# Backward chain of a recurrent-memory attention block: token-major output gradient by PE transposes in place of a transposing DMA

## The chip, the cores and the metric

The kernel runs on one core of one Trainium2 chip. The time is device microseconds of that core, one execution at a time. One run of the kernel before, 4074.3 us, counted as slow and is left out of the ratios. The experiments ran on several chips (11, 12 and 14 are on record); each ratio is to executions of the kernel before on the same chip in the same rounds. Readings by segment come from one profiled execution of each kernel.

The profile's names: PE is TensorE, which does the matmuls, PEld its weight loads, DVE is VectorE, ACT ScalarE, POOL GpSimd, and SP SyncE, which here only issues DMA. SBUF and PSUM are the core's memories; matmuls leave their results in PSUM, and an *evacuation* is the copy from there to SBUF. A `q` after an engine's name (SPq) is what its sequencer issues. The *span* is the time from the first to the last instruction.

## The reference

The reference computes one transformer block and all its gradients. The part that matters is the attention, which runs over 64 segments of 32 tokens, each with 8 memory rows that come from the segment before (cut to what matters):

```python
for s in range(n_seg):                                   # 64 segments, L = 8 + 32 = 40 rows
    h = jnp.concatenate([mem, xs], axis=1)
    q, k, v = (jnp.einsum('btd,dhe->bhte', h, W) for W in (Wq, Wk, Wv))   # 16 heads of 256
    p = _softmax(jnp.where(mask, (q @ k^T) * scale, -1e9))
    o = jnp.einsum('bhte,hed->btd', p @ v, Wo)
    mem = o[:, :M, :].copy()                             # goes to the next segment
```

So the backward pass is a chain as well: the gradient of segment s needs the memory gradient that segment s+1 leaves. Outputs are the block's result and nine gradients, within a tolerance on bf16 data.

## The kernel before

The kernel has four stages: forward chain (0 to about 1370 us), feed-forward (to about 1760), backward chain (to about 3200) and a tail that forms the weight gradients. One segment of the backward chain, in the order of the source (cuts marked with `...`; numbers are the lines that the profile shows):

```python
# 732: output gradient, head-major, 128 matmuls in 4 PSUM tiles
nc.tensor.matmul(pss[b][:, jj*L:(jj+1)*L], lhsT=WoT_sb[...], rhs=do_roll[:, kc, sl, :], ...)
for b in range(4):                                       # 75 on DVE, 77 on ACT
    k.evac(doT[:, 8*b:8*b+8, 0:L], ..., "vsvs"[b])
# 737: dO_sb, the token-major copy (transpose) of doT, two halves, by DMA on SP's queue
for hf in range(2):
    nc.sync.dma_start_transpose(out=dO_sb[:, 8*hf:8*hf+8, :],
                                in_=doT[:, 16*hf:16*hf+16, :].rearrange("p c n -> p (c n)"))
# 744: dP = dO V^T;  748 to 753: softmax gradient dS on DVE
# 711: three passes of 16 matmuls: "v" (needs dO_sb), "k" (needs dS, Q_sb), "q" (needs dS^T, K_sb)
# 761: 16 small transposes dS -> dS^T, before the "k" pass
# 775: 32 matmuls after each pass that add to the memory gradient
# 778 to 793: the memory gradient goes to do_roll for the next segment
...
if r == 0:       # r = s % 4; s falls, so this is the last of a tile of four segments
    for nm in "kqv":
        nc.gpsimd.dma_start(out=dr["X_" + nm][t], in_=blk[nm]...)   # 1 MB each
        nc.gpsimd.dma_start(out=dr["M_" + nm][t], in_=lo[nm]...)    # 0.25 MB each
    # 806 (96 matmuls), 811 and 817 (fp32, 4 each): DXN of the tile, off the chain
```

Every segment also loads V, Q and K of the next one with transposing DMAs (lines 683 to 685) on the same SP queue, each into a single buffer. The instructions of an engine are ordered by a scheduler when the kernel is built, so the order on PE is not simply that of the source. Below, "remainder r" means segments with s % 4 = r. The tile's stores are issued at remainder 0 and are on their way during the following segment, remainder 3.

## Time and profile before

| | before |
|---|---|
| median time | 4040.6 us (3 runs, 4034.8 to 4063.8) |
| backward chain, mean segment | 22.1 us |
| its granted PE clock, 1800 to 3180 us | 0.83 |
| PE idle in front of L711 for the transposing DMA | 176 us of 1380 |

The last row is the longest of PE's waits in that stretch (who waited for whom: us in total, times, longest):

```profile
PE psf L711 <- DMA arA<-arA: 176.0, 82, 17.5
```

From the page of the kernel before: busy time, the granted clock in 40 slices (tenths), the chain that ended last (by engine, then by line), and the group of the value pass (busy and mean; after the last bar, idle time before it and what ended it).

```profile
PE 3250.6 (81%) x54460; PEld 2063.5 (51%) x54526; DVE 1366.3 (34%) x2969; ACT 840.1 (21%) x2053; POOL 524.2 (13%) x1129
...
PEclk9999999998998699968888878788888888899999
...
PE 63%; DMA 19%; DVE 5%; issue 5%; SPq 4%; ACT 3%; POOL 1%; ACTq 0%; DVEq 0%; POOLq 0%
PE psf L382 11%; DMA arA<-arA 10%; PE po L775 10%; PE psf L899 7%; PE psf L732 4%; PE po L466 4%; PE psf L711 3%; PE fx L806 2%; PE psf L423 2%; ACT arA L77 2%; PE psf L569 2%; PE fx L495 2%; PE psf L782 2%; PE fx L904 2%; PE fx L363 2%
...
L711 PE MATMUL psf<-arB,arA 128*128 128x80 bf16 x1024 | 79.5, 243 | 194.6 <-DMA arA<-arA 194.3
```

`DMA arA<-arA` is the transpose from one SBUF place to another: doT to dO_sb. It holds 10% of the whole span, and practically all the idle time in front of the value pass is put down to it.

The busy times by stretch of the kernel before, for the body of the backward chain (columns: stretch, length, busy PE, PEld, DVE, ACT, POOL, then granted clock, DMA share, GB/s):

```profile
1800.00:3180.00 1380.00, 1107.20 (x22150) 718.88 (x22150) 465.96 (x1119) 293.38 (x916) 175.35 (x416) 0.83 0.75 148
```

The timeline of one segment of the kernel before (remainder 1; start, length, engine, line, then in brackets the idle time before it):

```profile
2443.25 4.21 PE L732 MATMUL psf<-arA,arW 128*128 128x40 bf16 x128 [0.28 <-DVE arA L786]
...
2445.87 3.36 SPq L737 DMA_TRANSPOSE arA<-arA  x2
...
2447.39 0.94 PE L744 MATMUL psf<-arA 128*64 128x40 bf16 x32
...
2448.95 0.46 PE L711 MATMUL psf<-arB,arA 128*128 128x80 bf16 x8 [0.62 <-DMA arA<-arA]
...
2449.99 0.74 PE L775 MATMUL po<-arW,arA 128*32 128x448 bf16 x9 [0.58 <-DVE arA L75]
...
2451.97 0.72 PE L711 MATMUL psf<-arB,arA 128*128 128x80 bf16 x8 [1.23 <-DMA arA<-arA]
```

PE ends the score-gradient matmuls at 2448.3 us, and the second half of the value pass starts at 2452.0. In between it has 17 matmuls to do.

The queue of SP in the kernel before, where a tile's stores are on their way (remainder 3 starts at 2484.7 us):

```profile
2481.61 7.90 SPq L685 DMA_TRANSPOSE arW<-KT  x1
2489.62 1.86 SPq L737 DMA_TRANSPOSE arA<-arA  x1
...
2492.90 1.46 SPq L737 DMA_TRANSPOSE arA<-arA  x1
```

The K load takes 7.9 us to be issued once, and the output gradient stands behind it.

Two measures recur below. Both are worked out from the instructions in the trace: the *period* of a segment, from the start of its first L732 matmul to that of the next segment's, and the *key start*, from the end of the last L732 matmul to the start of the first L711 matmul of the key pass. They are means over the segments that start after 1800 us.

### The profile page before, as it was taken

The numbers are of one execution on the slowest core, as the hardware profiler recorded it, in microseconds if no ns is written. First come the engines' busy times: TensorE is split into PE (matmuls) and PEld (weight loads), VectorE is DVE, ScalarE is ACT, GpSimd is POOL, SyncE is SP. The second block draws the span as 40 slices with busy tenths as digits, with TensorE's granted clock in tenths as the row PEclk, the third lists the DMA queues.
The fourth block names the chain that finished last, engine by engine and source line by source line (L and its number), as shares of the span: only waits on it lengthen the run. The fifth ranks groups of instructions, "written<-read, shape, count | busy, mean of one in ns | idle before, by whom it ended". The sixth has DMA issues, their size and how long they took to land.

```text
span 4023.1 us, 120689 instructions
## 1 busy us (share of the span) xinstructions
PE 3250.6 (81%) x54460; PEld 2063.5 (51%) x54526; DVE 1366.3 (34%) x2969; ACT 840.1 (21%) x2053; POOL 524.2 (13%) x1129
## 2 busy tenths in 40 slices
PE   4888988898888488838888788778887857899899
PEld 2666666666665365625555555445555523333444
DVE  3433443443343266713333333233333223110101
ACT  2222222222222132302222222122221100111100
POOL 3111111111111111111111111111111111000000
PEclk9999999998998699968888878788888888899999
DMA  7445444544543877897778776777787789867742
GB/s 258 154 147 170 155 147 157 162 150 145 175 142 125 198 181 177 203 228 141 151 148 160 166 142 149 131 140 149 153 156 167 203 270 184 178 137 155 182 167 83
DMA packets 1156999, 662.58 MB, mean 165 GB/s; under 512 B 1045316, under 2 KB 1075828, under 8 KB 1148740
## 3 DMA queue, kind: packets, MB, share of 16 engines
q1 hardware_dynamic: 1070148, 392.73, 47.7%
q0 software_dynamic: 58976, 238.56, 16.9%
q10 hardware_dynamic: 27360, 23.58, 2.0%
q8 instruction: 427, 7.00, 0.7%
q14 instruction: 88, 0.72, 0.1%
HBM read 124.49 MB, written 270.64 MB: 98 GB/s over the span
## 4 chain that ended last, share of the span: by engine, by line
PE 63%; DMA 19%; DVE 5%; issue 5%; SPq 4%; ACT 3%; POOL 1%; ACTq 0%; DVEq 0%; POOLq 0%
PE psf L382 11%; DMA arA<-arA 10%; PE po L775 10%; PE psf L899 7%; PE psf L732 4%; PE po L466 4%; PE psf L711 3%; PE fx L806 2%; PE psf L423 2%; ACT arA L77 2%; PE psf L569 2%; PE fx L495 2%; PE psf L782 2%; PE fx L904 2%; PE fx L363 2%
## 5 line engine op out<-in xcount | busy, mean ns | idle before, releaser
L75 DVE CAST arA<-psf 128x320 bf16<-128x320 f32 (+6 forms) x1093 | 498.5, 481 | 1246.7 <-PE psf L711 346.9
L77 ACT CAST arA<-psf 128x480 bf16<-128x480 f32 (+6 forms) x1139 | 442.8, 407 | 1883.8 <-PE psf L711 383.5
L775 PE MATMUL po<-arW,arA 128*32 128x448 bf16 x6144 | 442.6, 410 | 44.8 <-DVE arA L75 34.9
L382 PEld LDWEIGHTS <-arW 128*128 128x128 bf16 x16384 | 438.3, 98 | 30.8 <-issue 18.6
L382 PE MATMUL psf<-arA,arW 128*128 128x40 bf16 x16384 | 440.3, 182 | 16.2 <-issue 9.9
L732 PE MATMUL psf<-arA,arW 128*128 128x40 bf16 x8192 | 227.3, 183 | 62.2 <-POOL arA L680 37.8
L775 PEld LDWEIGHTS <-arA 128*32 128x32 bf16 x6144 | 163.0, 105 | 202.0 <-DVE arA L75 64.2
L732 PEld LDWEIGHTS <-arW 128*128 128x128 bf16 x8192 | 225.8, 98 | 77.4 <-issue 72.5
L899 PE MATMUL psf<-arW,arA 128*128 128x512 bf16 x990 | 258.5, 391 | 7.9 <-ACT arA L77 7.9
L899 PEld LDWEIGHTS <-arA 128*128 128x128 bf16 x1440 | 138.5, 100 | 206.8 <-issue 66.3
L711 PE MATMUL psf<-arB,arA 128*128 128x80 bf16 x1024 | 79.5, 243 | 194.6 <-DMA arA<-arA 194.3
L569 PE MATMUL psf<-arA,arW 128*128 128x256 bf16 x1344 | 167.4, 287 | 75.3 <-DMA arA<-arA 40.5
L75 DVE CAST arB<-psf 40x320 bf16<-40x320 f32 (+2 forms) x256 | 92.4, 361 | 310.5 <-PE psf L457 145.9
L569 PEld LDWEIGHTS <-arW 128*128 128x128 bf16 x1344 | 138.3, 103 | 106.4 <-issue 80.6
L711 PEld LDWEIGHTS <-arA 128*128 128x128 bf16 x1024 | 58.5, 123 | 254.6 <-DMA arA<-arA 232.1
L363 PE MATMUL fx<-arW,arA 128*128 128x512 bf16 x456 | 121.6, 388 | 58.0 <-DMA arW<-in_A_Wv_dram 39.0
L920 PE MATMUL psf<-arW 128*128 128x448 bf16 x450 | 103.0, 382 | 64.0 <-DVE arA L75 53.8
L466 PE MATMUL po<-arW,arB 128*8 128x448 bf16 x2048 | 149.0, 448 | 2.8 <-DVE arB L75 0.3
L423 PE MATMUL psf<-arW,arB 128*32 128x512 bf16 x2048 | 148.7, 381 | 1.2 <-issue 1.2
L806 PE MATMUL fx<-arW,arA 128*32 128x448 bf16 x1536 | 142.2, 396 | 0.0
L920 PEld LDWEIGHTS <-arW 128*128 128x128 bf16 x606 | 61.8, 103 | 129.8 <-issue 70.9
L457 PE MATMUL psf<-arB,arA 128*128 128x80 bf16 x1024 | 56.1, 217 | 89.3 <-DMA arA<-arA 73.8
(355 smaller groups left out, 3846.8 us busy)
## 6 DMA issues: line engine op xcount, KB each, us to landing
QT<-arA POOLq DMA_DIRECT2D x64, 512.0 KB, 3.8
KT<-arA SPq DMA_DIRECT2D x64, 512.0 KB
VG<-arA SPq DMA_DIRECT2D x64, 512.0 KB
X_o<-arA POOLq DMA_DIRECT2D x40, 512.0 KB, 4.8
Vx<-arA POOLq DMA_DIRECT2D x32, 512.0 KB, 3.2
arA<-Vx SPq DMA_DIRECT2D x128, 128.0 KB
X_v<-arA POOLq DMA_DIRECT2D x16, 1024.0 KB, 5.9
X_k<-arA POOLq DMA_DIRECT2D x16, 1024.0 KB, 8.0
```

What stands on the lines that cost most here:

```text
L75: nc.vector.tensor_copy(out=out, in_=in_)
L77: nc.scalar.copy(out=out, in_=in_)
L363: nc.tensor.matmul(pv[:, 0:512], lhsT=hx_b[t % 2][:, kc, :], rhs=Wv_sb[:, kc, n * 512:(n + 1) * 512], start=(kc == 0), stop=(kc == KC - 1))
L382: nc.tensor.matmul(pss[b][:, jj * L:(jj + 1) * L], lhsT=W_sb[:, kc, c * P:(c + 1) * P], rhs=hT_roll[:, kc, sl, :], start=(kc == 0), stop=( ...
L423: nc.tensor.matmul(pV[b][32 * j:32 * j + 32, 0:512], lhsT=memT_pad[:, kc, :], rhs=Wv_sb[:, kc, n * 512:(n + 1) * 512], start=(kc == 0), st ...
L466: nc.tensor.matmul(pO[32 * (j % 4):32 * (j % 4) + M, 0:D], lhsT=o8[:, j, :], rhs=Wo_sb[:, cj(j), :], start=(j < 4), stop=(j >= MC - 4), sk ...
L569: nc.tensor.matmul(ps[:, f2 * 256:(f2 + 1) * 256], lhsT=Wt[:, kc, c * P:(c + 1) * P], rhs=xT[:, kc, :], start=(kc == 0), stop=(kc == KC - 1))
L711: nc.tensor.matmul(ps[b][:, i * 2 * L:(i + 1) * 2 * L], lhsT=lhs[:, cl, :], rhs=rhs_bd[:, cl // 2, :, :].rearrange("p g n -> p (g n)"), st ...
L732: nc.tensor.matmul(pss[b][:, jj * L:(jj + 1) * L], lhsT=WoT_sb[:, kc, c * P:(c + 1) * P], rhs=do_roll[:, kc, sl, :], start=(kc == 0), stop ...
L775: nc.tensor.matmul(pH[32 * (j % 4):32 * (j % 4) + 32, 0:D], lhsT=blk[nm][:, j, r * SEG:(r + 1) * SEG], rhs=WT[:, cj(j), :], start=(wi == 0 ...
L806: nc.tensor.matmul(px[32 * (j % 4):32 * (j % 4) + 32, 0:D], lhsT=lo[nm][:, j, :], rhs=WT[:, cj(j), :], start=(wi == 0 and j < 4), stop=(wi ...
L899: nc.tensor.matmul(pa[2 * kc + g][:, 0:w], lhsT=lhs_of(b)[:, kc * P:(kc + 1) * P], rhs=rhs_of(b, g), start=(b == 0), stop=(b == nblk - 1), ...
```

## The change

The intent is to take the DMA out of the segment's chain: PE transposes doT itself, 8 blocks of 128x128 a half, into a PSUM tile of bf16, and ACT copies the tile to dO_sb. The consumers do not change.

```diff
-            for hf in range(2):
-                nc.sync.dma_start_transpose(out=dO_sb[:, 8 * hf:8 * hf + 8, :],
-                                            in_=doT[:, 16 * hf:16 * hf + 16, :].rearrange("p c n -> p (c n)"))
+
+            def token_major(hf):
+                ph = k.ps1()[:].bitcast(BF16)
+                for i in range(8):
+                    c0 = 2 * (8 * hf + i)
+                    nc.tensor.transpose(ph[:, i * P:(i + 1) * P], doT[:, c0:c0 + 2, :].rearrange("p c n -> p (c n)"), ident[:, :])
+                nc.scalar.copy(out=dO_sb[:, 8 * hf:8 * hf + 8, :], in_=ph.rearrange("p (c n) -> p c n", n=P))
+            token_major(0)
             pD = k.ps1()
             ...                       # 744 before, 749 after: the score-gradient matmuls
+            token_major(1)
```

Lines after the change move by 4 to 6: L744 becomes L749, L761 L767, L775 L781; the transposes are L741, their copies L742. L711 and L732 stay.

## The prediction

> **What bounds the kernel now.** 4040.6 us. The backward chain runs from about 1760 to 3200 us: 64 dependent segments, averaging 22.1 us. From 1800 to 3200 us the busy times by stretch show PE busy 1124 of 1400 us, a granted clock of 0.76 to 0.87 and a DMA share of 0.74 to 0.78. The chain of waits puts "DMA arA<-arA" at 10% of the span, and the groups show PE idle 194 us before L711 for that DMA. It is the transpose of the output gradient: its two halves are issued at L737 after the evacuations of L732, and the value pass (L711) needs them. From the timeline, the key pass starts 14.4, 10.7, 8.2, 8.3 us (means) after a segment's last L732 matmul, for segment number mod 4 of 3, 2, 1, 0. Remainder 3 is worst: the transposes queue behind the K load (7.9 us to issue once) while 3 MB of X_k, X_q and X_v are stored.
>
> **Removed.** Two DMA transposes a segment, 128 in all: about 2048 of some 8470 small packets a segment (an estimate: 3.2 us of the 16 engines). Their waits before L711 go.
>
> **Added.** 16 PE transposes a segment, like those of L883 in the tail (33.0 us for 384, so 86 ns each): 1.4 us of PE. Two ACT copies of 128x1024 bf16 from PSUM, 1.01 us each at L77 in the tail: 2.0 us of ACT, which is 21% busy. The shared PSUM tag gets two more users; I expect no stall there.
>
> **The new path**, after the last L732 matmul: 0.7 us transposes, 0.95 score-gradient matmuls, 0.7 transposes; the second copy ends near 3.4 us; the value pass ends near 4.0. The changed instruction order then has all 32 L775 matmuls (1.7 us) and the 16 dS transposes (0.6), so the key pass starts near 6.3 us. DVE has dS ready by about 5.2, before PE wants it. The rest of a segment (2.8 + 5.0 + 3.4 us) stays: 17 to 18 us for a plain one. Saved: about 2.2 us at remainders 0 and 1, 2.7 at remainder 2 (the DXN matmuls move later), 6.5 at remainder 3, keeping some stall for the K load. Mean 3.4 us over 63 segments: 215 us.
>
> **Clock.** The Trainium skill, "TensorE: Matmul & The Clock Gate", Part 1, has PE fall to half rate after idle windows of about 3.4 us; this trace agrees: its clock records are only 1.0 or 0.5, in multiples of 3.4 us, and segments at 0.91 lasted 18.2 to 20.3 us against 19.0 to 20.4 near 0.75. I expect 0.88 to 0.92 here; Part 4 says transposes do not count as busy, which could hold that back.
>
> **Predicted time:** 3822 us, 8 in 10 between 3760 and 3895. Faster by over 2%: 0.94; within 2%: 0.04; slower: 0.02.
>
> **What would show it.** The DMA entry leaves the top of the chain of waits; the key pass starts 6 to 6.6 us after L732 in plain segments; segments average 18.3 to 19 us; transposes take 60 to 90 ns, copies 1.0 us; q1 moves a quarter less in this stage; the backward granted clock rises; other phases stay within 10 us.
>
> **What would make it wrong.** The store burst at remainder 3 may delay the K, V or next-tile loads, returning part of the 6.5 us as another DMA wait; two ACT copies in a row may delay later evacuations; the clock may stay near 0.82; or less DMA traffic and a clock near 1 save more.

## The result

The changed kernel takes 3815.3 us (4 runs, 3808.7 to 3829.7), against 4037.7 for the kernel before on the same chip. The ratio is 0.9448, 95% interval 0.9391 to 0.9506: 5.5% faster. (A ratio is the mean time of one kernel's fast runs over that of the other's of the same rounds, so it is not quite the ratio of the medians quoted.)

From the page of the changed kernel, the same parts, and the group of the new copies:

```profile
PE 3141.8 (83%) x55484; PEld 2052.6 (54%) x55550; DVE 1350.1 (35%) x2969; ACT 960.6 (25%) x2181; POOL 522.8 (14%) x1129
...
PEclk9999999999998869996999989999999789999999
...
PE psf L382 11%; PE po L781 8%; PE psf L905 8%; PE psf L732 5%; PE po L466 4%; DMA arA<-arA 3%; PE psf L711 3%; PE psf L569 2%; PE fx L812 2%; PE psf L423 2%; PE fx L495 2%; PE fx L910 2%; PE fx L363 2%; PE psf L741 2%; PE psf L788 2%
...
L742 ACT COPY arA<-psf 128x1024 bf16<-128x1024 bf16 x128 | 129.5, 1012 | 55.6 <-PE psf L741 54.0
```

The DMA fell from 10% to 3% of the chain; what is left of that name belongs to other SBUF-to-SBUF transposes. PE has a thousand matmuls more and yet is busy 109 us less: the same matmuls take longer when the clock is lower. The 128 of L732 take 4.21 us in the segment shown of before, where the granted clock was half for 3.4 us, and 3.35 us in the one below, at full clock. The busy times by stretch, body of the backward chain, changed kernel:

```profile
1800.00:2954.00 1154.00, 996.15 (x23052) 707.24 (x23052) 450.20 (x1118) 409.86 (x1038) 174.61 (x415) 0.94 0.79 150
```

The clock rose from 0.83 to 0.94. The body is 226 us shorter (1380 to 1154): by these two lines PE is idle 115 us less and busy 111 us less. So about half of the gain came as shorter waits and half as less busy time, of which the higher clock is at least a part. No run here takes the waits away and keeps the clock low, so the two are not separated by experiment. The timeline of a plain segment of the changed kernel (remainder 1 again):

```profile
2359.90 3.35 PE L732 MATMUL psf<-arA,arW 128*128 128x40 bf16 x128
...
2363.10 0.61 PE L741 MATMUL psf<-ident,arA 128*128 128x128 bf16 x8
...
2363.63 0.69 PE L749 MATMUL psf<-arA 128*64 128x40 bf16 x32
2363.80 1.01 ACT L742 COPY arA<-psf 128x1024 bf16<-128x1024 bf16 x1
...
2364.26 0.62 PE L741 MATMUL psf<-ident,arA 128*128 128x128 bf16 x8
...
2364.86 0.46 PE L711 MATMUL psf<-arB,arA 128*128 128x80 bf16 x8
...
2364.97 1.01 ACT L742 COPY arA<-psf 128x1024 bf16<-128x1024 bf16 x1 [0.16 <-PE psf L741]
...
2366.03 0.46 PE L711 MATMUL psf<-arB,arA 128*128 128x80 bf16 x8 [0.71 <-ACT arA L742]
...
2366.43 1.70 PE L781 MATMUL po<-arW,arA 128*32 128x448 bf16 x32
```

The second half of the value pass starts 2.8 us after L732; in the segment shown of before it was 4.5. The only wait left in this piece is 0.7 us for the second ACT copy.

Where the time went, by remainder (mean periods in us):

| remainder | before | after | saved | saving predicted |
|---|---|---|---|---|
| 3 (the tile's stores on their way) | 26.4 | 24.3 | 2.1 | 6.5 |
| 2 | 22.4 | 16.7 | 5.7 | 2.7 |
| 1 | 19.7 | 16.2 | 3.5 | 2.2 |
| 0 | 19.9 | 16.7 | 3.2 | 2.2 |
| all | 22.1 | 18.4 | 3.7 | 3.4 |

From the first segment's start to the last one's, the chain took 1416.9 us before (1760.2 to 3177.2) and 1188.2 us after (1765.8 to 2954.0), 228.7 us less. The profiled spans differ by 216.5 us, since the chain begins 5.6 us later and what follows takes 6.7 us more.

The remainder-3 segments are the surprise: they kept nearly all their length. PE's waits in the body of the chain, changed kernel (who waited for whom: us in total, times, longest):

```profile
PE psf L732 <- issue: 39.2, 8, 12.7
PE psf L749 <- issue: 25.8, 3, 11.6
PE psf L711 <- ACT arA L742: 23.4, 34, 1.0
...
PE psf L741 <- issue: 8.8, 3, 4.6
PE psf L711 <- DMA arW<-QT: 5.7, 2, 4.1
...
PE psf L711 <- DMA arW<-KT: 3.9, 2, 3.1
```

The old wait of 176 us for the transposing DMA is gone. In its place, and at remainder 3 alone, stand stalls marked "issue": PE waits for nothing that the profile shows. One of them in the timeline of the changed kernel, at remainder 3, with SP's queue beside it:

```profile
2239.14 18.80 SPq L685 DMA_TRANSPOSE arW<-KT  x1
...
2244.92 0.94 PE L749 MATMUL psf<-arA 128*64 128x40 bf16 x27
...
2257.37 0.35 PE L749 MATMUL psf<-arA 128*64 128x40 bf16 x5 [11.52 <-issue]
...
2258.04 5.16 SPq L683 DMA_TRANSPOSE arA<-VG  x1
```

PE stops between two like matmuls of one group, after 27 of 32. The matmuls just before the stop already read the last quarter of doT, and V comes in one load, so an operand is hardly what it waits for there. Three facts of the trace point to the fetch of PE's own instructions. First, counting PE's instructions (weight loads too, and of a matmul and its load the one that starts first) from the start of the trace, 18 of the 23 PE gaps over 0.9 us in this stage end at a position that leaves the same remainder, 137, when divided by 256; the other five stand at a named operand. Second, each of the 18 ends 1.2 to 1.6 us after a 16 KB packet of the instruction queue landed, but for one, which ends 3.8 us after. Third, in front of the gap shown no packet of that queue starts between 2236.2 and 2254.8 us, where the 180 of this stage come 6.4 us apart on average; 180 times 256 is 46,080, and PE with its weight loads has 46,104 instructions there, so this queue carries PE's. The 18 add up to 82 us. The Trainium skill, "Runtime: NRT & Kernel Launch", section "Instruction fetch mechanics", says that instructions are refilled in 16 KiB blocks of 256 by a DMA queue of the sequencer's own, and that crossing a block is "mostly hidden". The block size agrees with this trace; "mostly hidden" does not hold while the stores are on their way. In the kernel before, such gaps add up to 21 us in 6 places: PE stood still at remainder 3 for the output gradient anyway (93 us of the 176).

### The profile page after: what moved, and what is told of

Its sections match the earlier page's. It is cut to its first block, busy times and chain, and to the rows that moved or that the text cites. A ratio compares the mean times of both kernels' runs of the same rounds, so it can differ in the third digit from the quotient of the medians.

```text
span 3806.6 us, 122548 instructions
## 1 busy us (share of the span) xinstructions
PE 3141.8 (83%) x55484; PEld 2052.6 (54%) x55550; DVE 1350.1 (35%) x2969; ACT 960.6 (25%) x2181; POOL 522.8 (14%) x1129
## 3 DMA queue, kind: packets, MB, share of 16 engines
q0 software_dynamic: 58976, 238.56, 18.4%
## 4 chain that ended last, share of the span: by engine, by line
PE 65%; DMA 14%; issue 7%; DVE 5%; SPq 4%; ACT 4%; POOL 1%; ACTq 0%; DVEq 0%; POOLq 0%
PE psf L382 11%; PE po L781 8%; PE psf L905 8%; PE psf L732 5%; PE po L466 4%; DMA arA<-arA 3%; PE psf L711 3%; PE psf L569 2%; PE fx L812 2%; PE psf L423 2%; PE fx L495 2%; PE fx L910 2%; PE fx L363 2%; PE psf L741 2%; PE psf L788 2%
## 5 line engine op out<-in xcount | busy, mean ns | idle before, releaser
L781 PE MATMUL po<-arW,arA 128*32 128x448 bf16 x6144 | 334.2, 360 | 42.5 <-DMA arW<-in_A_Wv_dram 21.2
L732 PE MATMUL psf<-arA,arW 128*128 128x40 bf16 x8192 | 225.7, 182 | 90.2 <-POOL arA L680 39.3
L732 PEld LDWEIGHTS <-arW 128*128 128x128 bf16 x8192 | 223.2, 98 | 107.1 <-issue 102.2
L905 PE MATMUL psf<-arW,arA 128*128 128x512 bf16 x990 | 260.8, 393 | 12.7 <-ACT arA L77 12.7
L905 PEld LDWEIGHTS <-arA 128*128 128x128 bf16 x1440 | 138.7, 100 | 213.6 <-issue 73.4
L781 PEld LDWEIGHTS <-arA 128*32 128x32 bf16 x6144 | 149.2, 97 | 176.4 <-DVE arA L75 44.1
L742 ACT COPY arA<-psf 128x1024 bf16<-128x1024 bf16 x128 | 129.5, 1012 | 55.6 <-PE psf L741 54.0
L457 PE MATMUL psf<-arB,arA 128*128 128x80 bf16 x1024 | 57.9, 221 | 97.3 <-DMA arA<-arA 77.5
L812 PE MATMUL fx<-arW,arA 128*32 128x448 bf16 x1536 | 121.8, 368 | 1.5 <-issue 1.5
L495 PE MATMUL fx<-arW,arA 128*128 128x448 bf16 x512 | 120.7, 362 | 0.0
```

What stands on the lines that cost most here:

```text
L495: nc.tensor.matmul(px[:, 0:D], lhsT=xblk[:, j, :], rhs=Wo_sb[:, cj(j), :], start=(j == 0), stop=(j == MC - 1))
L732: nc.tensor.matmul(pss[b][:, jj * L:(jj + 1) * L], lhsT=WoT_sb[:, kc, c * P:(c + 1) * P], rhs=do_roll[:, kc, sl, :], start=(kc == 0), stop ...
L781: nc.tensor.matmul(pH[32 * (j % 4):32 * (j % 4) + 32, 0:D], lhsT=blk[nm][:, j, r * SEG:(r + 1) * SEG], rhs=WT[:, cj(j), :], start=(wi == 0 ...
L812: nc.tensor.matmul(px[32 * (j % 4):32 * (j % 4) + 32, 0:D], lhsT=lo[nm][:, j, :], rhs=WT[:, cj(j), :], start=(wi == 0 and j < 4), stop=(wi ...
L905: nc.tensor.matmul(pa[2 * kc + g][:, 0:w], lhsT=lhs_of(b)[:, kc * P:(kc + 1) * P], rhs=rhs_of(b, g), start=(b == 0), stop=(b == nblk - 1), ...
```

## The experiments

Two questions: what of the change made the gain, and what holds remainder 3. For the first, the theory is latency: the DMA's way from doT to dO_sb was on the chain. Its rivals are the DMA traffic that the change takes away, the clock that busier PE keeps up, and the new instruction order that the scheduler makes.

### Dead DMA: the old traffic kept, without its latency

Edit on the changed kernel; nothing reads `spare`, which is free memory:

```diff
+            for hf in range(2):
+                nc.sync.dma_start_transpose(out=spare[:, 8 * hf:8 * hf + 8, :],
+                                            in_=doT[:, 16 * hf:16 * hf + 16, :].rearrange("p c n -> p (c n)"))
             def token_major(hf):
```

> The changed kernel, plus the two old DMA transposes of each segment into spare memory that nothing reads. Theory (the latency of the transposing DMA sat on the critical path): the time stays near the changed kernel's 3815 us, 3810 to 3880, plain segments (number mod 4 of 0 to 2) stay at 16.0 to 16.9 us; any loss falls in the remainder-3 segments. Rival (the gain came from less DMA traffic and a shorter SP queue): most of the 222 us is lost, 3960 to 4040 us, and plain segments go back to 18 us or more.

Measured: 3815.7 us (4 runs), ratio 0.9448 (0.9384 to 0.9511), the same as the changed kernel. Plain segments take 16.1 to 16.8 us, remainder 3 25.3. The stretch shows that the traffic was there, with a DMA share of 0.99 in place of 0.79:

```profile
1800.00:2960.00 1160.00, 988.35 (x22656) 696.00 (x22655) 442.54 (x1097) 401.60 (x1016) 173.07 (x411) 0.93 0.99 177
```

So taking some 3.2 us of DMA work (the prediction's estimate) out of each segment was worth nothing by itself, within the 0.6% that the interval leaves. The traffic rival falls.

### Dead PE work: the change's cost without its use

The mirror image, on the kernel before: the two DMA transposes stay and are waited for, and `token_major` writes `spare`.

```diff
+            # as in the change, but:
+                nc.scalar.copy(out=spare[:, 8 * hf:8 * hf + 8, :], in_=ph.rearrange("p (c n) -> p c n", n=P))
```

> The kernel before, plus the change's 16 PE transposes and two ACT copies a segment into spare memory that nothing reads; the value pass still waits for the DMA. PE's instruction order is then nearly that of the changed kernel. Theory (latency): no gain, 4010 to 4090 us, PE still idles over 150 us in front of L711 for the DMA. Rival (the added PE work keeps the clock up, or the new instruction order is what helps): 3820 to 3950 us and a backward clock of 0.9 or more.

Measured: 3976.4 us, ratio 0.9854 (0.9807 to 0.9900). This is a miss: 1.5% faster, where I expected nothing; the rival's 3820 to 3950 us did not come either. The wait for the DMA is all there, as PE's waits show for this run (stretch 1800 to 3100 us):

```profile
PE psf L712 <- DMA arA<-arA: 176.5, 95, 13.9
```

The granted clock rose to 0.89 in this stretch, from 0.83, with the wait still there. So busier PE and a higher clock, without an end of the wait, brought no more than these 1.5% here.

By remainder the gain is 3.3 us at 2 (22.4 to 19.1), 0.5 and 0.9 at 1 and 0, and none at 3. So about 60 of the 222 us do not come from the latency. Two causes of these 60 us remained: PE work or clock, or instruction order.

### One, two, three dead transposes: when the order changes

The same edit with N transposes and N*128 columns copied a half, in place of 8. With N=1 the order is nearly that of the kernel before. With N=2 the four fp32 transposes of DXN (L817 of before), which stand between the key pass and its rows in all 15 tiles, move behind the query pass, and one of the four DXN sums (L811) moves behind the dS transposes; four more of the L806 matmuls stand at remainder 2, in front of the second half of the value pass (15 in place of 11). From N=3 on the dS transposes follow all the value-pass rows, as in the changed kernel.

> The kernel before, plus 1 unused PE transpose and a 128-column ACT copy a half. The run with 2 gained 1.5%, nearly all at remainder 2 (22.4 to 19.9 us), where its instruction order has the four L817 transposes of DXN split and moved towards the next segment; with 1 transpose these stand in all 15 tiles where the kernel before has them, in front of the key pass's rows. If the place of the DXN work is the cause: no gain, 4015 to 4045 us, remainder 2 at 21.8 us or more. If any unused PE work does it (or the two more users of the PSUM tag): 3960 to 3995 us, remainder 2 near 20.

> The kernel before, plus 2 unused PE transposes (not 8) and a 256-column ACT copy for each half. With this little work the scheduler keeps the old instruction order (value-pass rows split around the dS transposes). If the 60 us that the run with all the unused work gained came from the new instruction order: no gain here, 4020 to 4060 us. If it came from the PE and ACT work as such (a busier PE, a higher clock): a part of it, 4005 to 4025 us.

> The same with 3 unused transposes a half: 6 of 16, but the scheduler now joins the dS transposes behind all the value-pass rows, as in the changed kernel. If instruction order is the cause: 3980 to 4005 us, and the step from 2 to 3 transposes is 20 to 50 us. If the PE work is the cause: within 12 us of the run with 2.

| N | ratio to before | 95% interval | remainder 2 |
|---|---|---|---|
| 1 | 0.9977 | 0.9938 to 1.0016 | 21.7 us |
| 2 | 0.9853 | 0.9817 to 0.9888 | 19.9 us |
| 3 | 0.9889 | 0.9857 to 0.9921 | 20.0 us |
| 8 | 0.9854 | 0.9807 to 0.9900 | 19.1 us |

(Medians 4022.2, 3968.4, 3985.5 and 3976.4 us.) The run with 2 went against what was written for it: I held it to be the old order, having looked only at the value-pass rows. Then I found that DXN had moved, and wrote the expectation of the run with 1 on that: it held for the time, and remainder 2 came out at 21.7 us, just under the 21.8 written. The run with 3 fell in its range, but the step of 20 to 50 us between 2 and 3 did not come (17 us the other way).

The step lies between 1 and 2, where PE's work hardly changes and the place of DXN does; more dead work adds nothing, and neither does joining the dS transposes. The order in which PE takes off-chain work is therefore the likely cause of the 60 us, mostly in the remainder-2 segment, where the end of DXN stands. The last column is from single executions, for N=2 the slowest of its six (4010.7 us) and for N=1 the fastest (3997.4), so the ratios weigh more.

How the order acts is not fully taken apart. In the traces PE idles 0.7 us less in a remainder-2 segment with N=2: L811's wait of 0.6 us for ACT is gone, and the wait for the DMA is no shorter (1.6 us before, 1.7 with N=2). The rest of the 2.4 us is less busy time: the clock rose there from 0.82 to 0.94.

### One half by DMA, the other by PE

```diff
 # e5: first half as in the change; in place of token_major(1), right after token_major(0):
+            nc.sync.dma_start_transpose(out=dO_sb[:, 8:16, :], in_=doT[:, 16:32, :].rearrange("p c n -> p (c n)"))
 # e6: second half as in the change; in place of token_major(0):
+            nc.sync.dma_start_transpose(out=dO_sb[:, 0:8, :], in_=doT[:, 0:16, :].rearrange("p c n -> p (c n)"))
```

> The changed kernel with the second half of the gradient (head chunks 8 to 15) made by the DMA transpose again, the first half by PE. Same DMA traffic as the next run. Theory (what counts is when each half arrives): this half is issued last, right after the last evacuation, so PE waits for it in every segment: plain segments 17 to 18.5 us in place of 16.0 to 16.9, remainder 3 back towards 25 to 27 us, total 3880 to 3965 us. Rival (cost in proportion to the DMA work): half of the gain lost, about 3925 us, in both half runs alike.

> The mirror image: first half by DMA, second half by PE. Theory: the first half is issued some 1.4 us before PE ends L732 and its latency hides behind the score-gradient matmuls and the remaining transposes; plain segments within 0.5 us of the changed kernel's 16.0 to 16.9; at remainder 3 the DMA still queues behind the K load, which adds some us there; total 3820 to 3895 us, clearly below the other half run. Rival: the same time as the other half run.

| | changed | second half DMA | first half DMA |
|---|---|---|---|
| median us | 3815.3 | 3911.6 | 3940.2 |
| ratio to before | 0.9448 | 0.9715 | 0.9756 |
| remainder 3 | 24.3 | 24.5 | 29.0 |
| remainder 2, 1, 0 | 16.7, 16.2, 16.7 | 18.6, 18.7, 18.4 | 17.5, 17.0, 17.5 |

The totals are alike, as the traffic rival had it, but the segments are not. With the second half by DMA every plain segment is about 2 us longer and remainder 3 no worse (I had written 25 to 27 us for it). There PE waits 60 us for the DMA, but its stalls marked "issue" fall from 85 to 25 us: one wait covers the other, as in the kernel before. With the first half by DMA the plain segments lose 0.8 us, as the theory has it for a DMA issued early (their medians lose 0.2 to 0.3), and remainder 3 loses 4.7. PE's waits of the run with the first half by DMA:

```profile
PE psf L711 <- DMA arA<-arA: 170.5, 62, 14.1
PE psf L732 <- issue: 37.3, 8, 9.7
```

My total for this run (3820 to 3895) was wrong: plain segments lost 0.8 us and not at most 0.5, and remainder 3 lost 4.7, which I had put at "some us". At remainder 3 PE waits 7.1 us a segment for the DMA, at most 13.0 (the 14.1 above is the chain's first segment, before any tile is stored). In the trace the half stands behind a K load that takes up to 17 us to be issued there. So the runs differ by when a half arrives and not by how much is moved, and the half that stands behind the K load during the burst arrives latest.

### Fewer stores: is remainder 3 the burst?

X_k, X_q, M_k and M_q are not stored, and the tail reads X_v and M_v in their place. The k and q weight gradients are wrong; the tail reads as many bytes as before.

```diff
-            for nm in "kqv":
+            for nm in "v":
                 nc.gpsimd.dma_start(out=dr["X_" + nm][t], ...)
```

> The changed kernel without the stores of X_k, X_q, M_k and M_q (the tail reads X_v and M_v in their place, so the k and q weight gradients are wrong on purpose): 1.25 MB instead of 3.75 MB stored at once per tile. Theory (the store burst starves instruction fetches and loads in the remainder-3 segments): those fall from a mean of 24.3 us to 17 to 18.5, the total to 3690 to 3745 us, and PE's stalls at one position of every 256 instructions go. Rival (the stall is the in-order SP queue or the single-buffered K, V and next-tile loads): over 3780 us, remainder 3 over 22 us.

> The same stores dropped from the kernel before. Theory (in the kernel before the burst acted by delaying the output-gradient transposes at remainder 3, and hid the fetch stalls behind that wait): remainder 3 falls from 26.4 us to 20 to 22, total 3925 to 3975 us. If the burst did not matter there: 4010 us or more.

| | stores as they are | fewer stores | remainder 3 |
|---|---|---|---|
| changed kernel | 3815.3 | 3696.8 (ratio 0.9169) | 24.3 to 16.6 us |
| kernel before | 4037.7 | 3908.5 (ratio 0.9712) | 26.4 to 18.9 us |

PE's waits in the changed kernel with fewer stores (1800 to 2850 us): the largest was there before, and of "issue" 1.7 us are left, the longest 0.9.

```profile
PE psf L711 <- ACT arA L742: 23.4, 36, 0.8
...
PE psf L711 <- issue: 0.9, 1, 0.9
```

The theory holds in both kernels: without the burst a remainder-3 segment is no longer than the others, the fetch stalls are gone, and the change itself is worth as much as with it (0.9169 over 0.9712 is 0.944). Both remainder-3 times came out under what I had written (17 to 18.5, and 20 to 22 us), and so did the total of the kernel before (3925 to 3975): the burst cost more than I thought. The rival, SP's in-order queue or the single buffers by themselves, falls: neither was touched.

### Spreading the stores

The same bytes, right results. X_k gets a second buffer (8 KB a partition, from free memory and by moving om2) and is stored two segments later, the three M stores three segments later. Moving the statements alone did not help in the build, where the scheduler issued a store as soon as its data were ready (no run here shows this). So a tiny DVE instruction that reads a value of the later segment, times zero, holds each one back.

```diff
-    blk = {nm: A(8 * i, 32, P) for i, nm in enumerate("kqv")}
+    blk_b = {"k": [A(40, 32, P), A(0, 32, P)], "q": [A(8, 32, P)] * 2, "v": [A(16, 32, P)] * 2}
-    om2 = A(40, 1024).bitcast(FP32)
+    om2 = B(5, 1024).bitcast(FP32)
...
+        def after_now(tl):
+            nc.vector.scalar_tensor_tensor(out=tl[:, 0, 0:1], in0=rsum[:, 0:1], scalar=0.0, in1=tl[:, 0, 0:1], op0=ALU.mult, op1=ALU.add)
+        for tp, go in ((t + 1, r == 2), (t, s == 0)):
+            if go and tp < NT:
+                after_now(blk_b["k"][tp % 2])
+                nc.gpsimd.dma_start(out=dr["X_k"][tp], in_=blk_b["k"][tp % 2].rearrange("p c n -> p (c n)"))
+        ...                                   # the same for the three M stores at r == 1
-            for nm in "kqv":                  # at r == 0
+            for nm in "vq":
```

> The changed kernel with the store burst spread: X_k from a second buffer, held back by a tiny DVE instruction until two segments later, the three M stores until three segments later; X_v and X_q as before. Same bytes, results right. Theory (the burst starves instruction fetch and loads at remainder 3): remainder 3 falls from 24.3 us to 17.5 to 20, the other segments gain at most 0.5, total 3715 to 3770 us. Rival (it is the total DMA work, not the burst): over 3800 us, the stalls move to other segments.

Measured: 3716.3 us (4 runs, 3703.9 to 3748.1), results right, ratio 0.9222 (0.9152 to 0.9293). This beats both kernels. Remainder 3 takes 18.9 us, the others 16.1 to 16.7, and the clock is 0.98. The DMA issues of the changed kernel, body of the chain (last column: median us from issue to landing):

```profile
X_v<-arA POOLq DMA_DIRECT2D x15, 1024.0 KB, 5.9
X_k<-arA POOLq DMA_DIRECT2D x15, 1024.0 KB, 15.3
X_q<-arA POOLq DMA_DIRECT2D x15, 1024.0 KB, 15.9
```

and of the kernel with spread stores:

```profile
X_v<-arA POOLq DMA_DIRECT2D x15, 1024.0 KB, 5.9
X_q<-arA POOLq DMA_DIRECT2D x15, 1024.0 KB, 6.8
X_k<-arA POOLq DMA_DIRECT2D x15, 1024.0 KB, 6.6
```

The DMA share is 0.75, hardly below the 0.79 of the changed kernel: it was the burst and not the total. Of the stalls at one remainder of 256, 26 us are left, in 11 places.

### Two tries that gained nothing

The second copy from PSUM on DVE, with the value pass's evacuations on ACT:

```diff
-                nc.scalar.copy(out=dO_sb[:, 8 * hf:8 * hf + 8, :], in_=ph.rearrange("p (c n) -> p c n", n=P))
+                k.evac(dO_sb[:, 8 * hf:8 * hf + 8, :], ph.rearrange("p (c n) -> p c n", n=P), "sv"[hf])
 ...                     # and, for "v" alone, the engines of the value pass's evacuations
```

> The changed kernel with the second copy from PSUM on DVE (0.69 us measured for such a copy) in place of ACT, and the value pass's evacuations moved to ACT to make room. If the two ACT copies in a row are what PE waits for (0.7 us in plain segments), the value pass ends 0.3 to 0.5 us sooner, plain segments 15.5 to 15.8 us, total 3780 to 3800 us. If DVE's softmax-gradient chain is the limit instead: no change or up to 30 us slower.

Measured: 3826.7 us, ratio 0.9474 (0.9395 to 0.9552), no gain; plain segments 16.3 to 16.8 us. At remainder 2 the value pass did end 0.25 us sooner, and the next segment started no sooner; at remainders 1 and 0 it ended 0.1 us later. The 0.7 us in front of the second half is not worth anything as the other engines stand.

The spread kernel with Wv loaded before Wk and Wq at the chain's start:

```diff
-    for (Wsrc, WT) in ((k.Wk2, WkT_sb), (k.Wv2, WvT_sb), (k.Wq2, WqT_sb)):
+    for (Wsrc, WT) in ((k.Wv2, WvT_sb), (k.Wk2, WkT_sb), (k.Wq2, WqT_sb)):
```

> The changed kernel with spread stores, and the transposing load of Wv issued before that of Wk and Wq at the chain's start, since the value pass is what needs a weight first; PE idles 20.8 us there for Wv in the spread kernel. Expected: the wait falls to 5 to 15 us, and 3700 to 3712 us against 3716 for the spread kernel; no gain if the queue drains too slowly for the order to matter.

Measured: 3719.0 us, ratio 0.9220 (0.9186 to 0.9254), the same as the spread kernel. The wait of 20.8 us for Wv became one of 10.5 us for Wk and one of 6.5 for Wv, once at the start: 17.0 us, where I expected 5 to 15. A gain of 4 us is within the noise here.

## Why the prediction was right

The prediction was 3822 us; 3815 was measured. Its mechanism held: the waits for the DMA went, and what stood between was cheap. But its terms by segment were off in opposite directions and nearly cancelled, so that the total came this close is luck.

- *"Their waits before L711 go"*: right. 176 us of waits fell to zero for this DMA, and dead traffic in its place cost nothing, so it was latency and not load. Of the 222 us, about 60 came from elsewhere (below), which leaves about 160 for the latency and the clock that rose with its end (0.9854 to 0.9448 of 4036 us; an estimate, as if the two parts simply add).
- *PE transposes at 86 ns, key start near 6.3 us:* too slow. Eight took 0.53 us from the first start to the start of the next group (66 ns each) at full clock, and the key pass starts 5.1 us after L732 in nearly every plain segment. The score-gradient matmuls took 0.63 us to the next group in place of 0.95, and the dS transposes 0.31 in place of 0.6. Plain segments took 16.2 to 16.7 us, not 17 to 18. Of the 3.5 and 3.2 us saved at remainders 1 and 0 (2.2 predicted), 1.7 and 1.8 are idle time of PE; the rest is less busy time, for which the prediction had no term; the higher clock is at least a part of it.
- *Saved at remainder 2: 2.7 us:* mis-sized; it was 5.7. I charged the moved DXN matmuls as a cost. The runs with 2 and with 8 dead transposes show the new order gaining 2.4 and 3.3 us there while the DMA is still waited for.
- *Saved at remainder 3: 6.5 us:* mis-sized; it was 2.1. I had named the store burst as a risk and kept "some stall for the K load". What came was mostly another wait, PE's instruction fetch, 82 us over the stage, that the old wait had covered. Over some 16 segments this term was about 70 us too hopeful and the three others together about 85 us too low.
- *Clock 0.88 to 0.92:* it was 0.94, and 1.0 in most plain segments. The Trainium skill, "TensorE: Matmul & The Clock Gate", Part 1, holds for the two rates and the window: the records are 1.0 or 0.5 only, in multiples of 3.4 us, and 92 of 120 us at half rate are now at remainder 3, where PE still stands still. That the window before a fall is idle, as the prediction took it from the page, this trace does not show: in the body of the kernel before, the 72 falls to half rate each end a window of 3.4 us in which PE was busy 77% at most (48% in the median), and only 7 of them one in which it was busy less than 5%. So a window with some idle time in it was enough. Part 4 says that the clock gate does not count transposes as busy. Runs of 0.6 us of them, twice a segment, did not hold the clock down; whether they were counted, no run here shows.
- *q1 moves a quarter less; other phases within 10 us:* right. q1 had about 8500 packets of 256 bytes a segment and now some 6500; the other phases moved by 5.6 and 6.7 us.

## What to carry to other kernels

A transpose through DMA that stands between two steps of a dependent chain costs its latency each time (2.8 us of waiting a segment here), even where its traffic costs nothing; a PE transpose with a copy can be cheaper even where PE is the busiest engine, and here PE's clock rose as well when the waits went, from 0.83 to 0.94. When a wait is taken away, look for what was hidden behind it: here a burst of stores that delays loads and, past them, PE's own instructions; stalls marked "issue" that recur at one position of every 256 instructions were its sign, and spreading the stores by a data dependency was the cure (3815 to 3716 us). Any edit lets the scheduler order the rest anew, so a control with the added work left unused is worth its run: about a quarter of this gain was order, as far as these runs tell (60 of 222 us).

## What the Trainium skill lacked or had wrong

- "Runtime: NRT & Kernel Launch", "Instruction fetch mechanics", has the refill of a block "mostly hidden". Beside a burst of 3.75 MB of stores it was not: 18 stalls of up to 12.7 us, 82 us in all, and none over 0.9 us without two thirds of the burst. No page that I read warns of data DMA delaying instruction fetch, or names the sign of it.
- "TensorE: Matmul & The Clock Gate", Part 4, gives a 128x128 bf16 transpose about 275 ns in a kernel. The profile's mean for one is 229 ns here, but that is not what a row of them costs: within a group of eight they start about 56 ns apart, and a group takes 0.53 us to the start of the next (66 ns each).
- The same Part says that a copy by DVE is needed after a PE transpose. An ACT copy served as well here: 1.01 us for 128x1024 bf16 on ACT, and moving the second one to DVE gained nothing.
- Part 1 of that page gives no share of busy time below which a window brings the half rate. In the body of the kernel before it came after windows of up to 77% busy PE, and full rate came back after windows of 81% and more; in the changed kernel 20 of 23 falls were below 80%, three at 92%. So busy time alone does not settle it.
